# A 1-D convolution by Winograd points on one core: inputs laid out by channel blocks, output kept transposed, another order at the start

## The chip, the cores and the metric

The kernel runs on one core of a Trainium2 chip. TensorE (PE) multiplies matrices into PSUM, which has 8 banks of 512 fp32 values for each of 128 partitions. VectorE (DVE) and ScalarE (ACT) read PSUM; GpSimd (POOL) works on SBUF alone. SyncE (SP), ScalarE and GpSimd can issue DMAs. The metric is the device time of one execution in microseconds (us), the median of several runs.

## The reference

```python
B, S, C = 2, 2048, 1024          # x: (B, S, C), w: (3, C, C), all bf16
xp = jnp.pad(x, ((0, 0), (1, 1), (0, 0)))
y = sum(jnp.einsum('bsc,cd->bsd', xp[:, k:k + S, :], w[k]) for k in range(3))
y = (y - mean) * (g * (1.0 / jnp.sqrt(var + 1e-5))) + b
return jax.nn.silu(y)
```

It is a convolution of width 3 along the sequence with full channel mixing, then a normalization with given statistics and a SiLU.

## The kernel before

The convolution is computed in blocks of R = 6 output rows from NJ = 8 input rows by a Winograd scheme with eight points. For each batch, the sequence gives NB = 342 blocks. Three things are needed.

*Inputs.* A window of 128 rows of x, all 1024 channels, is loaded by `load_x` (L119, 2 KB for each row) and multiplied on TensorE by a small matrix `rm`. One matmul takes one window and one block of 128 channels and gives 8 points x 21 blocks = 168 columns, with the channels on the partitions. `t_job` (L314) does six or four such matmuls into two banks and has them evicted to `T_sb` by ScalarE (L333) or VectorE (L335), whichever its running estimates in `clock` say is done first. There are 17 windows for each batch and 8 channel blocks (`CT`). The matrix `rm` itself is built by some 20 small VectorE instructions (`transform_matrix`), the scale and bias of each channel come through four DMAs of GpSimd and a transpose.

*Weights.* For each block of 128 output channels (`dc`, 8 of them) the three taps w0, w1, w2 are combined to six tensors `u`: points 1 and 2 are (w0 + w2) plus and minus w1, points 3 and 4 (w0 + 4 w2) plus and minus 2 w1, points 5 and 6 (4 w0 + w2) plus and minus 2 w1. GpSimd does the last additions (L188, two for each pair), the sums come from VectorE (L169) or GpSimd (L167, L216, L225, L243), the doubled or quadrupled taps from ScalarE (L155, L237) or GpSimd. Points 0 and 7 (called 0 and inf) use w0 and w2 as they are ("raw", `wch` in the profile's names).

*Products.* A `Unit` (L344) is one output-channel block of one batch; there are 16, in the order (dc 0, batch 0), (dc 0, batch 1), (dc 1, batch 0) and so on. `product` (L361) is one point: 8 matmuls of 342 columns, one for each input-channel block, accumulated in one bank. A unit uses four banks, 0 to 3 or 4 to 7 in turn. `run` (L473) multiplies points 1, 3, 2, 4, 5, 6. Behind point 1, 3 and 5 ScalarE copies the bank to SBUF (`copy`, L380 and L382), since the next point that belongs to the pair is accumulated onto the same bank: point 2 onto point 1, 4 onto 3, 6 onto 5. VectorE then forms the sums and differences (`combine`, L387) into a few SBUF tiles and into the banks. At last points 0 and inf, the raw ones, are accumulated onto banks 0 and 3, and ScalarE applies scale, bias and SiLU (L394) into `yT`, which has the channels on the partitions.

The order of each engine's instructions is the order in which the program issues them (`manual_schedule` on all five engines). `run` has seams, `behind(1)` to `behind(6)`, at which work of other units is placed: the list `also` gives pairs of a seam and a function. `rest` (L465) puts the end of the unit before there: in the steady state the inner SiLUs and the product inf behind point 5, so between the matmuls of point 5 and point 6, and the product 0 behind point 6. The third unit (i = 2) has product 0 behind point 4 and inf behind point 5.

The first unit is special (`run_first`, L420): it multiplies points 0, 1, 3, 2, 4, 5, 6, and between its matmuls, at places given by the list `at` of `Between`, the transforms of batch 1 are issued into banks 4, 6 and 1. Its point inf and its SiLUs follow in the second unit (`rest_first`).

*Output.* A finished `yT` is turned by a DMA transpose (`turn`) and stored by seven DMAs on SP's queue. At the end the last unit is split into two halves of 214 and 128 blocks; there the transposes are done on TensorE (`put`, L530) and evicted (L531), and the products 0 and inf of the first half lie between points 5 and 6 of the second half and behind them.

Of the kernel before, what the change touches and what calls it, by code (L numbers as in the profile page):

```python
# [12 lines left out]
I32 = mybir.dt.int32  # L13
# [5 lines left out]
W0_AT = (5, 8, 16)  # L19
EARLY = 23  # L20
XBUFS = 12
T_FIRST = 21500.0
WARM = 2
WT = 21

@with_exitstack
def kernel(
    ctx: ExitStack,
    tc: tile.TileContext,
    x: bass.AP,  # L30
    w: bass.AP,
    mean: bass.AP,
    var: bass.AP,
    g: bass.AP,
    b: bass.AP,
# [3 lines left out]
    B, S, C = x.shape  # L39
    D = w.shape[2]  # L40
    CT, DC = C // P, D // P
    NB = -(-S // R)
    NW = -(-NB // WT)
    LAST = NB - WT * (NW - 1)
    assert S % P == 0 and NB <= 512
# [3 lines left out]
    wpool = ctx.enter_context(tc.tile_pool(name="wpool", bufs=1))  # L49
# [7 lines left out]
    opool = ctx.enter_context(tc.tile_pool(name="opool", bufs=2))  # L57
    xwin_scope = ExitStack()
    xpool = xwin_scope.enter_context(tc.tile_pool(name="xpool", bufs=XBUFS))
# [8 lines left out]
    rows = consts.tile([4 * DC, P], BF16, name="rows")  # L68
    zeros = consts.tile([P, 512], FP32, name="zeros")
    nc.vector.memset(zeros, 0.0)  # L70
    for _ in range(WARM):
        nc.tensor.matmul(ps[:, 7], lhsT=zeros[:, 0:P], rhs=zeros, start=True, stop=True)
# [4 lines left out]
    def transform_matrix():  # L77
        v = nc.vector
        val = consts.tile([P, 3, WT], I32, name="val")
        nc.gpsimd.iota(val, pattern=[[1, 3], [-R, WT]], base=-1, channel_multiplier=1)  # L80
        m = consts.tile([P, 4, 3, WT], FP32, name="m")
        f = consts.tile([P, 3, 2, WT], FP32, name="f")
        c = consts.tile([P, 2, WT], FP32, name="c")
        rm = consts.tile([P, NJ, WT], BF16, name="rm")
        m0, m2, m4, m6 = (m[:, q] for q in range(4))
        for q, coef in ((1, -8.0), (2, 1.0), (3, 1.0), (0, 36.0)):
            v.tensor_scalar(m[:, q], val, float(2 * q), coef, op0=ALU.is_equal, op1=ALU.mult)
        for k, (c4, c6) in enumerate(((34.0, -8.0), (40.0, -32.0), (10.0, -2.0))):
            v.scalar_tensor_tensor(out=f[:, k], in0=m4[:, 1:3], scalar=c4, in1=m2[:, 1:3], op0=ALU.mult, op1=ALU.add)
        v.scalar_tensor_tensor(out=c, in0=m6[:, 0:2], scalar=-36.0, in1=m0[:, 0:2], op0=ALU.mult, op1=ALU.add)  # L90
        for k, (c4, c6) in enumerate(((34.0, -8.0), (40.0, -32.0), (10.0, -2.0))):
            v.scalar_tensor_tensor(out=f[:, k], in0=m6[:, 1:3], scalar=c6, in1=f[:, k], op0=ALU.mult, op1=ALU.add)
        v.scalar_tensor_tensor(out=c, in0=m4[:, 0:2], scalar=189.0, in1=c, op0=ALU.mult, op1=ALU.add)
        f1, f2, f3 = (f[:, k] for k in range(3))
        for j, a0, s0, a1, op in (
            (1, f1[:, 0], 1.0, f1[:, 1], ALU.add), (2, f1[:, 0], 1.0, f1[:, 1], ALU.subtract),
            (3, f2[:, 1], 2.0, f2[:, 0], ALU.add), (4, f2[:, 1], -2.0, f2[:, 0], ALU.add),
            (5, f3[:, 0], 2.0, f3[:, 1], ALU.add), (6, f3[:, 0], 2.0, f3[:, 1], ALU.subtract),
            (0, m2[:, 1], 23.625, c[:, 1], ALU.add), (7, m2[:, 0], -23.625, c[:, 0], ALU.subtract),
        ):  # L100
            v.scalar_tensor_tensor(out=rm[:, j], in0=a0, scalar=s0, in1=a1, op0=ALU.mult, op1=op)
        return rm

    rm = transform_matrix()

    clock = {"pe": 3500.0, "act": 0.0, "dve": 0.0, "dma": 3600.0}
    cost = {"act": (0.833, 250.0), "dve": (1.042, 215.0)}
    bank_free = {}

    def ends(e, size):  # L110
        return max(clock[e], clock["pe"] + 100.0) + cost[e][0] * size + cost[e][1]

    def busy(e, size):
        clock[e] = ends(e, size)

    order = [NW - 1] + list(range(2, NW - 1)) + [0, 1]
    xwin = {}

    def load_x(bi, wi):  # L119
        xw = xpool.tile([P, C], BF16, name="xw")  # L120
        lo = max(R * WT * wi - 1, 0)
        hi = min(lo + P, S)
        nc.sync.dma_start(out=xw[0:hi - lo, :], in_=x[bi, lo:hi, :])  # L123
        clock["dma"] += 5.4 * (hi - lo)
        xwin[bi, wi] = xw, clock["dma"]

    w_all = w.rearrange("k (ct p) d -> p k ct d", p=P)
    raw, wts = {}, {}

    wpools = {0: wpool}  # L130

    def load_w(pair, k, half=None):

        if (pair, "tile") not in raw:
            raw[pair, "tile"] = wpools[pair % 2].tile([P, 3, CT, 2, P], BF16, name=f"wch{pair % 2}")
        wch = raw[pair, "tile"]
        h0, h1 = (0, 2) if half is None else (half, half + 1)
        cols = slice((2 * pair + h0) * P, (2 * pair + h1) * P)
        nc.sync.dma_start(
            out=wch[:, k, :, h0:h1].rearrange("p c h d -> p c (h d)"), in_=w_all[:, k, :, cols]  # L140
        )
        clock["dma"] += 1400.0 * (h1 - h0)
        for h in range(2):
            raw[2 * pair + h] = wch[:, :, :, h]

    double, sums, act_work, dve_work = {}, {}, [], []
# [5 lines left out]
    def double_w(dc, eng):  # L152
        t = spool.tile([P, CT, P], BF16, name="w1x2")
        if eng is nc.scalar:
            nc.scalar.mul(t, raw[dc][:, 1], 2.0)  # L155
            busy("act", CT * P)
        else:
            eng.tensor_scalar(t, raw[dc][:, 1], 2.0, 0.0, op0=ALU.mult, op1=ALU.add)
        double[dc] = t

    def even_part(dc, q, eng, by=None):

        w0, w2 = raw[dc][:, 0], raw[dc][:, 2]
        e = epool.tile([P, CT, P], FP32, name=f"e{q}")
        f, h = (w2, w0) if q == 1 else (w0, w2)
        if q == 0:
            eng.tensor_tensor(e, w0, w2, op=ALU.add)  # L167
        elif eng is nc.vector:
            eng.scalar_tensor_tensor(out=e, in0=f, scalar=4.0, in1=h, op0=ALU.mult, op1=ALU.add)  # L169
        else:  # L170
            t = spool.tile([P, CT, P], BF16, name="w1x2")
            if by is nc.scalar:
                by.mul(t, f, 4.0)
                busy("act", CT * P)
            else:
                by.tensor_scalar(t, f, 4.0, 0.0, op0=ALU.mult, op1=ALU.add)
            eng.tensor_tensor(e, t, h, op=ALU.add)
        if eng is nc.vector:
            busy("dve", CT * P)
        sums[dc, q] = e  # L180

    def transform_w(dc, q, signs=(0, 1)):

        o = double[dc] if q else raw[dc][:, 1]
        if (dc, q) not in wts:
            wts[dc, q] = upool.tile([P, 2, CT, P], BF16, name=f"u{q}")
        for i in signs:
            nc.gpsimd.tensor_tensor(wts[dc, q][:, i], sums[dc, q], o, op=(ALU.add, ALU.subtract)[i])  # L188

    def prepare_w(dc):  # L190

        even_part(dc, 0, nc.gpsimd)
        transform_w(dc, 0)

        def second():
            even_part(dc, 1, nc.vector)
            transform_w(dc, 1)

        def third():
            even_part(dc, 2, nc.vector)  # L200
            transform_w(dc, 2)

        act_work.append(lambda: double_w(dc, nc.scalar))
        dve_work.extend((second, third))

    def prepare_first(dc):


        w0, w2 = raw[dc][:, 0], raw[dc][:, 2]
        g, f = (spool.tile([P, CT, P], BF16, name="w1x2") for _ in range(2))  # L210
        nc.gpsimd.tensor_scalar(f, w0, 4.0, 0.0, op0=ALU.mult, op1=ALU.add)
        for q, t, h in ((0, w0, w2), (1, g, w0)):
            if q:
                nc.gpsimd.tensor_scalar(g, w2, 4.0, 0.0, op0=ALU.mult, op1=ALU.add)
            sums[dc, q] = epool.tile([P, CT, P], FP32, name=f"e{q}")
            nc.gpsimd.tensor_tensor(sums[dc, q], t, h, op=ALU.add)  # L216

        def left():
            transform_w(dc, 0, (0,))
            double_w(dc, nc.scalar)  # L220
            transform_w(dc, 1, (0,))
            transform_w(dc, 0, (1,))
            transform_w(dc, 1, (1,))
            sums[dc, 2] = epool.tile([P, CT, P], FP32, name="e2")
            nc.gpsimd.tensor_tensor(sums[dc, 2], f, w2, op=ALU.add)  # L225
            transform_w(dc, 2)

        return left

    def prepare_second(dc):  # L230

# [3 lines left out]
        def times4(tap):  # L235
            t = spool.tile([P, CT, P], BF16, name="w1x2")
            nc.scalar.mul(t, tap, 4.0)  # L237
            busy("act", CT * P)
            return t

        def even(q, t, h):
# [102 lines left out]
    class Unit:  # L344

# [383 lines left out]
```

## Time and profile before

| What | us |
|---|---|
| median of 3 runs (lowest, highest) | 187.62 (187.03, 187.85) |
| span of the profiled execution | 185.5 |
| PE busy | 178.0 |
| DVE busy | 153.0 |
| ACT busy | 112.9 |
| POOL busy | 146.8 |

The span goes from the first to the last instruction or landing that the profiler recorded. An engine's busy time is the union of its instructions; matmuls overlap each other, so the distance between their starts tells more than their own duration (299 ns for a spacing of about 145 ns). "Idle before, releaser" is the idle time ahead of an instruction and what ended it. Tile names such as `T_sb`, `u`, `wch`, `pc`, `ps` are those of the code. A line of a listing in order of time has the start, the length from the first to the last of the merged instructions, engine, line, operation, output and input, and a count. A line of windows has the stretch, its length, and for PE, weight loads, DVE, ACT and POOL the busy time and the number of instructions, then the granted clock, the DMA engines' busy share and GB/s.

### The profile page before, as it was taken

What the parts mean: (1) busy time and instruction counts of PE and PEld (TensorE: products, weight loads), DVE (VectorE), ACT (ScalarE), POOL (GpSimd) and SP (SyncE); (2) the same over time, 40 slices, a digit from 0 to 9 for tenths busy, and PEclk for the clock granted to TensorE, in tenths of its full rate; (3) what the DMA queues carried; (4) which work ended last, traced back from release to release, by engine and by line L of the source; (5) the groups of instructions that cost most, each with busy time, mean ns of one, the idle gap of its engine ahead of it and who ended that gap; (6) DMA issues with size and microseconds to landing.
All of it is one profiled execution on the core that took longest, in us unless ns stands there. A gap on an engine that the chain in (4) does not pass through costs nothing.

```text
span 185.5 us, 3732 instructions
## 1 busy us (share of the span) xinstructions
PE 178.0 (96%) x1403; PEld 125.9 (68%) x1403; DVE 153.0 (82%) x214; ACT 112.9 (61%) x183; POOL 146.8 (79%) x89
## 2 busy tenths in 40 slices
PE   6889999999999999999999999999999999999991
PEld 2678688866666666666666666666666666669890
DVE  5278777997668999999988998879988997678792
ACT  3589888896638565456545654565456546363791
POOL 7099899999998879999999999999999973020120
PEclk9999999999999999999999999999999999999998
DMA  5999999065426855698859557995583968766845
GB/s 166 326 344 328 377 386 252 7 203 143 79 48 62 183 106 134 198 200 187 161 114 206 109 135 156 217 211 108 136 178 80 209 57 203 151 139 134 196 96 113
DMA packets 88046, 31.72 MB, mean 171 GB/s; under 512 B 75659, under 2 KB 83866, under 8 KB 88028
## 3 DMA queue, kind: packets, MB, share of 16 engines
q1 hardware_dynamic: 86860, 31.24, 72.3%
q10 hardware_dynamic: 848, 0.20, 0.5%
q8 instruction: 11, 0.18, 0.4%
q0 software_dynamic: 320, 0.03, 0.2%
q14 instruction: 7, 0.06, 0.1%
HBM read 14.82 MB, written 8.39 MB: 125 GB/s over the span
## 4 chain that ended last, share of the span: by engine, by line
PE 85%; DMA 5%; DVE 4%; ACT 2%; SPq 1%; issue 0%; DVEq 0%; ACTq 0%
PE ps L369 79%; DMA xw<-in_x_dram 5%; PE ps L322 5%; DVE T_sb L335 3%; SPq L123 1%; ACT T_sb L333 1%; PE ps L530 1%; DVE sd L387 0%; DVE o L531 0%; ACT outer L394 0%; DVEq L335 0%; ACTq L333 0%
## 5 line engine op out<-in xcount | busy, mean ns | idle before, releaser
L369 PE MATMUL ps<-T_sb,u 128*128 128x342 bf16 (+2 forms) x816 | 120.1, 299 | 0.1
L369 PEld LDWEIGHTS <-u 128*128 128x128 bf16 x816 | 76.8, 97 | 33.4 <-issue 0.2
L188 POOL TENSOR_TENSOR u<-e,w1x 128x1024 bf16<-128x1024 f32 x32 | 69.4, 2191 | 3.9 <-DVE e L169 2.5
L369 PE MATMUL ps<-T_sb,wch 128*128 128x342 bf16 (+2 forms) x272 | 42.6, 299 | 0.4 <-ACT T_sb L333 0.4
L394 ACT ACTIVATE yT<-ps,beta,scale 128x342 bf16<-128x342 f32 (+4 forms) x49 | 33.5, 713 | 13.3 <-PE ps L369 13.3
L387 DVE SCALAR_TENSOR_TENSOR t<-ps,sd 128x684 f32<-128x684 f32 (+2 forms) x51 | 39.1, 822 | 0.6
L188 POOL TENSOR_TENSOR u<-e,wch 128x1024 bf16<-128x1024 f32 x16 | 38.5, 2424 | 1.2 <-DMA wch<-in_w_dram 0.7
L369 PEld LDWEIGHTS <-wch 128*128 128x128 bf16 x272 | 25.7, 97 | 11.9 <-issue 0.6
L380 ACT COPY pc<-ps 128x342 f32<-128x342 f32 (+2 forms) x35 | 14.9, 426 | 28.7 <-PE ps L369 28.4
L333 ACT CAST T_sb<-ps 128x1008 bf16<-128x1008 f32 (+2 forms) x31 | 25.6, 874 | 7.4 <-PE ps L322 7.1
L335 DVE CAST T_sb<-ps 128x1008 bf16<-128x1008 f32 (+2 forms) x19 | 20.7, 1116 | 10.4 <-PE ps L322 10.3
L387 DVE SCALAR_TENSOR_TENSOR ps<-ps,t 128x684 f32<-128x684 f32 (+2 forms) x34 | 28.3, 832 | 0.6
L169 DVE SCALAR_TENSOR_TENSOR e<-wch 128x1024 f32<-128x1024 bf16 x12 | 26.2, 2182 | 0.0
L322 PE MATMUL ps<-rm,xw 128*128 128x168 bf16 (+2 forms) x272 | 25.0, 237 | 1.0 <-ACT T_sb L333 0.3
L322 PEld LDWEIGHTS <-xw 128*128 128x128 bf16 (+2 forms) x272 | 20.9, 100 | 6.4 <-issue 3.7
L387 DVE SCALAR_TENSOR_TENSOR ps<-ps,pc 128x342 f32<-128x342 f32 (+2 forms) x34 | 16.9, 497 | 9.2 <-PE ps L369 7.8
L167 POOL TENSOR_TENSOR e<-wch 128x1024 f32<-128x1024 bf16 x7 | 16.9, 2409 | 0.4 <-DMA wch<-in_w_dram 0.4
L394 ACT ACTIVATE yT<-t,beta,scale 128x684 bf16<-128x684 f32 (+2 forms) x17 | 15.7, 924 | 0.0
L387 DVE SCALAR_TENSOR_TENSOR t<-ps,t 128x684 f32<-128x684 f32 (+2 forms) x17 | 13.9, 818 | 0.0
L589 POOL DMA_DIRECT2D out_dram<-o x2 | 1.3, 659 | 15.6 <-DMA o<-yT 15.6
L387 DVE SCALAR_TENSOR_TENSOR sd<-pc,ps 128x342 f32<-128x342 f32 (+2 forms) x17 | 8.2, 485 | 6.2 <-ACT sd L380 6.1
L380 ACT COPY sd<-ps 128x342 f32<-128x342 f32 (+2 forms) x17 | 7.3, 428 | 9.7 <-PE ps L369 9.1
(62 smaller groups left out, 61.8 us busy)
## 6 DMA issues: line engine op xcount, KB each, us to landing
xw<-in_x_dram SPq DMA_DIRECT2D x32, 256.0 KB
out_dram<-o SPq DMA_DIRECT2D x28, 192.0 KB
wch<-in_w_dram SPq DMA_DIRECT2D x8, 512.0 KB
wch<-in_w_dram SPq DMA_DIRECT2D x8, 256.0 KB
out_dram<-o SPq DMA_DIRECT2D x14, 120.0 KB
out_dram<-o SPq DMA_DIRECT2D x3, 128.0 KB
o<-yT SPq DMA_TRANSPOSE x15
out_dram<-o SPq DMA_DIRECT2D x12, 7.5 KB
```

The costliest lines, as they stand in the source:

```text
L123: nc.sync.dma_start(out=xw[0:hi - lo, :], in_=x[bi, lo:hi, :])
L167: eng.tensor_tensor(e, w0, w2, op=ALU.add)
L169: eng.scalar_tensor_tensor(out=e, in0=f, scalar=4.0, in1=h, op0=ALU.mult, op1=ALU.add)
L188: nc.gpsimd.tensor_tensor(wts[dc, q][:, i], sums[dc, q], o, op=(ALU.add, ALU.subtract)[i])
L322: nc.tensor.matmul(v[:, q, c], lhsT=xw[0:rows, (c0 + c) * P:(c0 + c + 1) * P], rhs=mat[0:rows, :, 0:n], start=True, stop=True,)
L333: nc.scalar.copy(dst, src)
L335: nc.vector.tensor_copy(dst, src)
L369: nc.tensor.matmul(self.bank[q], lhsT=lhsT, rhs=T_sb[self.bi][:, ct, j, nsl], start=not add and ct == 0, stop=ct == CT - 1, skip_group_che ...
L380: nc.scalar.copy(dst, self.bank[q])
L387: nc.vector.scalar_tensor_tensor(out=out, in0=in0, scalar=scalar, in1=in1, op0=ALU.mult, op1=op1)
L394: nc.scalar.activation(dst, src, ACT.Silu, bias=beta[:, dc:dc + 1], scale=scale[:, dc:dc + 1])
L530: nc.tensor.transpose(v[:, a, q], src, ident)
```

## The change

The arrays are laid out on the host before the launch, with no arithmetic beyond padding and the constant matrix: x as windows by batch and channel block, so that one channel block of 16 windows (512 KB) is one DMA with 4 KB for each partition; the last 48 rows of each batch apart (`xl`); w by output-channel block with 6 KB for each partition (2 KB for one tap); the four parameter vectors as one array; and the transform matrix as an input. The output stays as the device writes it, (batch, dc, channel, row in block, block), and is put in order on the host.

On the device, a transform job (`Jobs.do`) is now one channel block and six or four windows, so batch 0 is transformed channel block by channel block, through all eight banks in four pairs; batch 1 uses three pairs. While batch 0 is awaited, short matmuls of zeros (`keep_busy`) may be issued. The first unit (`First`) uses banks 0 and 1 for points 0, inf, 1, 3, 2, 4 (0 and inf are copied to `kept` and added later), then bank 2 for points 5 and 6; its matmuls and the transforms of batch 1 are issued in the order in which the running estimates say that they can start. Its point 6, its last combinations and its three SiLUs, from SBUF tiles, are placed in the second unit, at seams 1 to 4, together with ScalarE's scalings of the taps of dc 1 (`prepare_second`) at seams 1, 2 and 4. The third unit has both raw products at seam 4. Each unit's `yT` is stored by one DMA. The end has no transposes, and the inner SiLUs of the first half stand at seam 3 of the second half. In unchanged functions (`product`, `copy`, `combine`, `run`) the instructions are the same.

```diff
+    def keep_busy(until, bank):
...
+        z = zeros.bitcast(BF16)
+        n = 384 if clock["pe"] > WARM_AT else 192
+        while clock["pe"] + 200.0 < until:
+            nc.tensor.matmul(ps[:, bank, 0:n], lhsT=z[:, 0:P], rhs=z[:, 0:n], start=True, stop=True)
+            matmuls(n)
...
+        def evens():
+            even(dc, 0, w0, w2)
+            g = scaled(w2, 4.0, nc.gpsimd)
+            even(dc, 1, g, w0)
...
         def left():
+            double_w(dc, nc.vector)
...
+            for q, i in ((0, 0), (1, 0), (0, 1), (1, 1)):
+                transform_w(dc, q, (i,))
...
+            f = scaled(w0, 4.0, nc.gpsimd)
+            even(dc, 2, f, w2)
...
+            for i in range(2):
+                transform_w(dc, 2, (i,))
...
     def prepare_second(dc):
...
         def second():
+            even(dc, 1, scaled(w2, 4.0, nc.scalar), w0)
         def third():
             double_w(dc, nc.scalar)
             transform_w(dc, 1)
         def fourth():
+            even(dc, 2, scaled(w0, 4.0, nc.scalar), w2)
             transform_w(dc, 2)
...
+    class Jobs:
+        def __init__(self, bi):
...
+            self.todo = [(None, 0, 0)] + [
+                (ct, f, min(6, NF - f)) for ct in range(CT) for f in range(0, NF, 6)
+            ]
...
+        def place(self):
...
+            slots = [(4, 5), (6, 7), (2, 3)]
+            if not self.bi:
+                slots += [(0, 1)]
...
+    class First(Unit):
...
+            self.todo = [
+                (j, q, add, ct) for j, q, add in (
+                    (0, 0, False), (NJ - 1, 1, False), (1, 1, False), (3, 0, False), (2, 1, True), (4, 0, True),
+                    (5, 2, False), (6, 2, True),
+                ) for ct in range(CT)
+            ]
...
+        def at(self):
...
+            if q == 2 and jobs[1]:
+                return float("inf")
+            return max(u, t_at[self.bi, ct], bank_free.get(q, 0.0))
...
+        def finish(self):
+            while self.todo:
                 self.do()
+            b2, b3 = self.bank[2:]
+            self.combine(b3, b2, -0.5, self.p[5])
+            for t, a in zip(self.t, (-1.6, -0.4, -0.1)):
+                self.combine(t, self.high, a, t)
...
+        def rest(self, between):
+            return [(1, self.finish)] + [(q + 2, lambda q=q: self.silu(slice(2 * q, 2 * q + 2), self.t[q])) for q in range(3)]
...
+    load_small(0)
+    load_x(0, 0, 2)
+    for ct in range(1, CT):
+        load_x(0, ct)
+        if ct in W0_AT:
+            load_w(0, ((0, 2, 1)[W0_AT.index(ct)],))
...
+    while jobs[0]:
+        slot, ready = jobs[0].place()
+        keep_busy(ready, slot[0])
+        jobs[0].do()
...
+    unit = First(0, 0)
+    while jobs[1] or unit.todo[0][0] != 6:
+        if left and clock["dve"] > raw_at[0, 1] - 500.0:
+            left.pop()()
+        at = jobs[1].place()[1] if jobs[1] else None
+        if at is not None and (not unit.todo or at <= max(clock["pe"], unit.at())):
+            jobs[1].do()
+        else:
+            unit.do()
...
+        also = prev.rest(quiet)
+        if i == 1:
+            also = [(1, second[1]), (2, second[2]), (4, second[3])] + also
+        if i == 2:
+            also = prev.rest(quiet, 4, 4)
...
+        if bi == 0 and dc + 3 < DC:
+            load_w(dc + 3, (0, 1, 2))
+        prev.store(nc.sync)
...
+    h0.run(quiet, prev.rest(quiet, 5, 5))
+    prev.store(sp)
+    h1 = Unit(dc, bi, 0, 0, H)
+    h1.run(quiet, [(3, h0.silu_inner)])
+    h0.store(sp, inner)
+    h0.product(3, NJ - 1, True, quiet)
+    h0.product(0, 0, True, quiet)
+    h1.product(0, 0, True, quiet)
+    h1.product(3, NJ - 1, True, quiet)
+    h0.silu(outer, ps[:, h0.b0:h0.b0 + 4:3, H:NB])
     h1.silu_inner()
+    h1.silu(0, h1.bank[0])
+    h1.silu(R - 1, h1.bank[3])
+    h0.store(sp, outer)
+    h1.store(sp, slice(0, R - 1))
+    h1.store(ac, slice(R - 1, R))
```

More of the change, by code (lines that the diff above doesn't have):

```diff
@@ L104 @@
[L104 to L144, printed above, removed]
@@ L146, with ends, busy, landed @@
-    double, sums, act_work, dve_work = {}, {}, [], []
+    clock = {"pe": 3400.0, "act": 3200.0, "dve": 1500.0, "pool": 2500.0, "dma": 2300.0}
+    cost = {"act": (0.833, 170.0), "dve": (1.042, 155.0), "pool": (2.0, 80.0)}
+    def ends(e, size, ready):
+        return max(clock[e], ready) + cost[e][0] * size + cost[e][1]
+    def busy(e, size, ready=None):
+        clock[e] = ends(e, size, clock["pe"] + 250.0 if ready is None else ready)
+        return clock[e] + 100.0
+    def landed(nbytes):
+        left = nbytes
+        slow = max(0.0, 8200.0 - clock["dma"]) * 255.0
+        at = min(left, slow)
+        clock["dma"] += at / 255.0 + (left - at) / 410.0
+        return clock["dma"] + 100.0
@@ new lines, in matmuls, with load_small @@
+    def matmuls(cols):
+        clock["pe"] += cols / (2.34 if clock["pe"] > WARM_AT else 1.18)
+    def keep_busy(until, bank):
[4 more added lines that the diff above has]
+            matmuls(n)
+    xt, xt_at, raw, raw_at = {}, {}, {}, {}
+    small, small_at = {}, {}
+    def load_small(bi):
+        t = xpool.tile([P, NF, P], BF16, name="xw").rearrange("p f c -> p (f c)")
+        nc.sync.dma_start(out=t[0:LROWS, 0:CT * P], in_=xl[bi])
+        small[bi], small_at[bi] = t, landed(LROWS * CT * P * 2)
@@ new lines, in load_x, with load_w @@
+    def load_x(bi, ct, parts=1):
+        t = xpool.tile([P, NF, P], BF16, name="xw")
+        xt[bi, ct], xt_at[bi, ct] = t, []
+        step = NF // parts
+        for q in range(parts):
+            s = slice(q * step, (q + 1) * step)
+            nc.sync.dma_start(out=t[:, s], in_=x[bi, ct, :, s])
+            at = landed(P * step * P * 2)
+            xt_at[bi, ct] += [at] * step
+    def load_w(dc, taps):
+        if dc not in raw:
+            raw[dc] = wpools[dc // 2 % 2].tile([P, 3, CT, P], BF16, name=f"wch{dc // 2 % 2}")
+        if len(taps) == 3:
+            nc.sync.dma_start(out=raw[dc], in_=w[dc])
+        else:
+            for k in taps:
+                nc.sync.dma_start(out=raw[dc][:, k], in_=w[dc, :, k])
+        for k in taps:
+            raw_at[dc, k] = landed(P * CT * P * 2)
@@ L204, in prepare_w, with pool @@
         dve_work.extend((second, third))
+    def pool(n=1):
+        clock["pool"] += n * 2130.0
+        return clock["pool"]
+    u_at = {}
     def prepare_first(dc):
         w0, w2 = raw[dc][:, 0], raw[dc][:, 2]
[L210 to L216, printed above, removed]
@@ L344, with quiet @@
+    def quiet():
+        pass
+    yts = [ypool.tile([P, R, NB], BF16, name=f"yT{q}") for q in range(B)]
     class Unit:
@@ L705 @@
[L705 to L709 removed]
+    inner, outer = slice(1, R - 1), slice(0, R, R - 1)
+    h0 = Unit(dc, bi, 4, H, NB)
+    h0.run(quiet, prev.rest(quiet, 5, 5))
[6 more added lines that the diff above has]
+    h1.product(0, 0, True, quiet)
```

577 lines of the change are left out of this document (209 added, 368 removed), and 8 rows, old and new, of the table _POINTS.

## The prediction

> **What bounds the kernel now.** I read the page first, then the chain that ended last, then windows, and then the order of time around the seams. The page says that TensorE is busy nearly always, at the full granted clock:
>
> ```profile
> PE 178.0 (96%) x1403; PEld 125.9 (68%) x1403; DVE 153.0 (82%) x214; ACT 112.9 (61%) x183; POOL 146.8 (79%) x89
> PEclk9999999999999999999999999999999999999998
> ```
>
> The chain shows from where on it is the bound alone: 952 matmuls in one piece from 37.44 us. What can be won or lost lies before that piece and behind it. A load takes 5.54 us from issue to landing while the queues are full, and eight 128-wide matmuls at the end take 0.45.
>
> ```profile
> 8.13 5.54 DMA xw<-in_x_dram
> ...
> 37.44 136.02 PE ps L369 x952
> ...
> 179.80 0.45 PE ps L369 x8
> ...
> 180.95 0.57 ACT outer L394
> ```
>
> The window over the middle gives the pace (691 records touch it, some 689 start in it: 100/689 = 0.1451 us for a 342-wide matmul); two single microseconds give the loading rate with x alone in 2 KB rows (387 GB/s) and with weights in 512 B rows (274).
>
> ```profile
> 60.00:160.00 100.00, 100.00 (x691) 66.85 (x690) 91.85 (x110) 54.21 (x92) 90.50 (x39) 1.00 0.75 155
> 24.00:25.00 1.00, 1.00 (x13) 0.81 (x12) 0.54 (x1) 0.99 (x2) 1.00 (x1) 1.00 1.05 387
> 29.00:30.00 1.00, 1.00 (x14) 0.90 (x13) 0.61 (x1) 1.00 (x3) 0.92 (x2) 1.00 1.22 274
> ```
>
> Last, ScalarE and GpSimd in the second unit. See the spacing of ScalarE's instructions (a copy 0.35, a doubling 0.96, a SiLU of 684 elements 0.85) and that its copy of point 5 has only 0.35 us of slack; GpSimd's last line ends the second channel block's weights, at 53.16.
>
> ```profile
> 36.79 0.45 ACT L380 COPY pc<-ps 128x342 f32<-128x342 f32 x1 [0.42 <-PE ps L369]
> 36.55 0.89 PE L322 MATMUL ps<-rm,xw 127*128 127x168 bf16 x10
> 37.29 7.13 PE L369 MATMUL ps<-T_sb,u 128*128 128x342 bf16 x48
> 42.52 1.06 ACT L237 ACTIVATE w1x<-wch 128x1024 bf16<-128x1024 bf16 x1
> 43.48 0.62 ACT L394 ACTIVATE yT<-ps,beta,scale 128x342 bf16<-128x342 f32 x1
> 44.45 0.44 ACT L380 COPY pc<-ps 128x342 f32<-128x342 f32 x1 [0.35 <-PE ps L369]
> 46.15 0.95 ACT L394 ACTIVATE yT<-t,beta,scale 128x684 bf16<-128x684 f32 x1
> 48.94 4.22 POOL L188 TENSOR_TENSOR u<-e,w1x 128x1024 bf16<-128x1024 f32 x2
> 54.70 7.13 PE L369 MATMUL ps<-T_sb,u 128*128 128x342 bf16 x48
> ```
>
> **The mark.** Both kernels issue the same 1088 product matmuls and 272 transform matmuls. I count to one mark M, the first matmul of point 6 in the third unit: in both orders 168 products and all transforms lie before it. Before, M is 54.70. Behind it lie 792 wide matmuls (792 x 0.1451 = 114.9) and 48 narrow ones of the first half unit (0.09 each, 4.3): 119.2. Then 0.45 for eight transposes, and 11.04 from there (174.46) to the end: 185.4, against the profiled span of 185.5. The median of the runs is 187.62, so 2.1 us lie around the span; I keep them.
>
> **Start: loading.** Removed are the matrix built on VectorE, two identity matmuls, the parameter transposes and one fp32 warm-up: all end before 9 us, beside the first loads, and cost nothing now. The two new small DMAs on ScalarE's queue must land before the first transform; the nearest rows, GpSimd's small loads, land 3.3 to 5.1 us after issue. Late by 1 us, the transforms still catch up, as tiles 6 and 7 arrive last: 0. The eleven filler matmuls that the planner's list gives fit gaps; the last costs 0 to 0.2.
>
> The last tile of batch 0 has 4.87 MB through its end (4.29 of x, two weight taps, small ones). The first 4 us move 0.58 MB (53, 182 and 344 GB/s). Rows of 2 KB at 387 and 512 B at 274 mean 0.085 and 0.030 us on one of 16 engines; in a straight line 4 KB takes 0.157, an estimate of 416 GB/s. So 4 + 0.52/0.387 + 3.77/0.416 = 14.4 for the bytes. The load in the chain above landed 1.5 to 2.2 us after the bytes ahead of it had passed: 16.3 (15.9 to 16.6; at the mean rate of before up to 18).
>
> [...]
>
> First product: six matmuls 0.44, latency 0.25, ScalarE's eviction 1.01 (its row), 0.1: 18.1. From there to the end of point 5: 56 products, 8.1, and 128 transforms of 0.0725, 9.3 (batch 1). The corresponding stretch of before (19.61 to 37.44) took 1.4 more than its work; I keep 1.4 (0.5 to 2.5: evictions, two new copies, one more combination and the doubling on VectorE, which no row shows: between the 0.69 of a 1024-element copy and the 2.18 of the fp32 sum; I take 0.7, the nearest in kind). End of point 5: T = 36.9. The same 56 products end at 38.45 in before, 112 matmuls ahead of M. **Won: 1.5.**
>
> **Second and third unit: ScalarE.** Times now from T. The second unit puts on ScalarE, between its first copy and the copy of point 5: scaling of a tap, copy, doubling, SiLU, copy, SiLU, another scaling, SiLU. Before had neither the first scaling (done earlier) nor the three wide SiLUs there. The first copy starts at 1.41 (point 1, 8 x 0.1451 + 0.25), the scaling at 1.76; the next copy waits for point 3 until 3.73 (point 6 of the first unit now lies between). Then with the spacings shown: doubling 4.10, SiLU 5.07, copy 5.93, SiLU 6.28, scaling 7.14, SiLU 8.11, copy of point 5 8.97 to 9.41. Point 6 adds into the bank that this copy reads, so TensorE waits until 9.47; its own work brings it there at 6.97. **Lost: 2.5**, if the SiLUs' inputs are there: VectorE ends them at 3.9, 4.7 and 5.5. Queued behind the SiLUs are those very copies; nothing else of ScalarE waits.
>
> The third unit now runs both raw-weight products ahead of point 5, none between 5 and 6. The cover of its copy is gone: 0.25 + 0.44 + 0.06 = **0.75 lost**. The 36.55 to 37.29 rows show this wait: point 5 ends at 36.55, the copy runs 36.79 to 37.24, point 6 starts at 37.29, and ten transforms filled it. So M = 36.9 + 112 x 0.1451 (16.25) + 3.25 = 56.4.
>
> GpSimd gives a floor for M. Its chain from the first u to the last of the second channel block ran 19.24 to 53.16, plus a scaling of 1.1 now inside: 35.0. It starts when tap 2 (3.82 MB, 11.9 + 1.8) plus 5.5 of sums is done: 19.2. M is not before 54.2, so GpSimd isn't reached.
>
> **Middle.** The same instructions. Fifteen DMA transposes and the block stores go from SP's queue, one 525 KB store per unit comes; it queues behind a weight load that waits for the unit's raw products, but its tile is next written some 15 us later. Cost 0. The 15.6 us that GpSimd waited for transposes held nobody.
>
> **End.** From the end of the first half's point 6 (0): eight transposes less before it (0.45 won). Points 1, 3, 2, 4, 5 of the last half take 0.45 each, 0.13 wait for a copy: 2.4. The first half's inner SiLUs now stand ahead of the copy of point 5, and need VectorE until 2.27: the copy ends at 3.5, point 6 at 4.0 (1.2 wait, where before other products and transposes lay). Two products of 0.72, two of 0.45: TensorE ends at 6.3. ScalarE from 5.68: 0.61, 0.51, 0.46, 0.37, 0.46: 8.1. The last store: before took 3.0 from its issue (182.48, second of two) for 64 KB; 32 KB alone, between that and the 2.1 of the smallest: 2.75. 10.85 in place of 11.04. **Won: 0.65.**
>
> Sum: 56.4 + 119.2 + 10.85 = 186.45, against 185.4 by the same count: +1.05, and 188.7 for the median.
>
> **Rivals.** (1) Faster: loading ends so early that GpSimd's floor takes the place of ScalarE's wait. For it speaks that no row shows 4 KB rows; against it, that evictions then limit. With the tile at 15.0 and 0.5 of waits T is 34.7 and M 54.2: 184.3, so 186.5. It decides by itself from T below 34.9. Chance 0.17. (2) No change: the tile at 16.0, waits of 0.8 and a store of 2.4 give T 36.0, M 55.5, the end at 185.2: 187.4. 0.28. (3) The start gains nothing: the tile at 17.5 and waits of 2 give T 38.7, M 58.2: 188.3, so 190.5. 0.15. (4) The forecast, with waits of 1.3 to 2.3: 188.6 to 189.6. 0.40. [...]
>
> 0.5% (0.94 us) is about what these runs can tell from no change. Slower 0.40 + 0.15, same 0.28, faster 0.17. The range 185.9 to 190.5 reaches from most of (1) to (3); the forecast's own stands with it.
>
> **What would show it.** The first wide product near 18 and T near 37; TensorE idle for 2.5 us in the second unit with ScalarE's copy ending it, 0.75 in the third; M near 56.4; TensorE ending some 1.8 us ahead of ScalarE at the end. The prediction falls if the second unit shows no such wait, if T lies below 35, or if GpSimd's weights end the wait in the third unit.

## The result and the profile after

The changed kernel takes 193.93 us, the median of 4 runs (192.45 to 194.83), against 187.43 for the kernel before, run beside it. The ratio is 1.034, with a 95% interval of 1.029 to 1.039. Slower was forecast, but by 0.6%; 188.7 us and the range up to 190.5 were both too low. The profiled execution took 194.4 us with a span of 192.6; it was forecast by the same count at 186.45. So 6.15 us of that execution have to be explained, and they fall in three places. (Two of the kernels below have one run over 1.5% above their fastest, 195.25 and 188.58; it is left out of their medians and ratios.)

Two lines of the page of the changed kernel: PE's busy time is no longer than before (176.9 against 178.0), though the span is 7.1 us longer, and one digit in the row of the granted clock, the eleventh of 40, just behind a quarter of the span, is a 6.

```profile
PE 176.9 (92%) x1373; PEld 125.1 (65%) x1373; DVE 150.9 (78%) x192; ACT 109.0 (57%) x175; POOL 139.4 (72%) x73
PEclk9999999999699999999999999999999999999995
```

The chain that ended last in the changed kernel (start, length, what). TensorE's one piece of before, 136 us from 37.44, has become two: 64 matmuls from 47.75 and 840 from 59.40. The 840 are the middle and the first half unit, as long as predicted. The 64 should take 64 x 0.1451 = 9.3 us and took 11.08. The last SiLU ends at 184.24 + 2.35 = 186.59; the span ends 6.0 us later.

```profile
47.75 11.08 PE ps L340 x64
...
58.90 0.46 ACT pc L349
59.36 0.04 issue
59.40 119.51 PE ps L340 x840
...
182.12 2.09 PE ps L340 x24
184.21 0.02 issue
184.24 2.35 ACT yT L361 x5
```

Windows of the changed kernel; the last three columns are granted clock, DMA share and GB/s. Four things are to be seen. Loads of x in 4 KB rows moved 413 GB/s. From 48 to 51 us TensorE ran at a clock of 0.50: five or six matmuls touch each microsecond in place of nine in the window behind. The middle has the 691 records of before. At the end the bytes of the last stores are through soon after 188, and then nothing moves for 4 us, although the span isn't over.

```profile
10.00:14.00 4.00, 3.95 (x49) 3.44 (x47) 3.84 (x4) 3.62 (x6) 0.00 (x0) 1.00 1.03 413
48.00:49.00 1.00, 1.00 (x5) 0.59 (x4) 0.27 (x1) 0.00 (x0) 1.00 (x1) 0.50 0.79 320
49.00:50.00 1.00, 1.00 (x6) 0.47 (x4) 0.00 (x0) 0.00 (x0) 1.00 (x2) 0.50 0.51 205
50.00:51.00 1.00, 1.00 (x5) 0.58 (x4) 0.67 (x2) 0.00 (x0) 1.00 (x1) 0.50 0.00 0
51.00:52.00 1.00, 1.00 (x9) 0.60 (x7) 1.00 (x2) 0.12 (x1) 0.92 (x2) 0.96 0.04 8
60.00:160.00 100.00, 100.00 (x691) 66.84 (x690) 92.39 (x110) 53.18 (x91) 92.11 (x41) 1.00 0.27 88
...
187.00:188.00 1.00, 0.00 (x0) 0.00 (x0) 0.00 (x0) 0.00 (x0) 0.00 (x0) 0.81 0.70 173
188.00:189.00 1.00, 0.00 (x0) 0.00 (x0) 0.00 (x0) 0.00 (x0) 0.00 (x0) 0.50 0.11 24
189.00:190.00 1.00, 0.00 (x0) 0.00 (x0) 0.00 (x0) 0.00 (x0) 0.00 (x0) 0.50 0.00 0
```

The second unit in order of time, first ScalarE of the changed kernel. It is the queue that the prediction wrote down: copy, scaling, copy, doubling, SiLU, copy, SiLU, scaling, SiLU, copy. Only the second scaling did not start right behind the SiLU, but waited 0.48 until GpSimd had ended a sum at 45.43.

```profile
39.27 0.45 ACT L349 COPY pc<-ps 128x342 f32<-128x342 f32 x1 [1.01 <-PE ps L340]
39.61 1.06 ACT L145 ACTIVATE w1x<-wch 128x1024 bf16<-128x1024 bf16 x1
41.55 0.46 ACT L351 ACTIVATE pc<-ps 128x342 f32<-128x342 f32 x1 [0.87 <-PE ps L340]
41.90 1.05 ACT L145 ACTIVATE w1x<-wch 128x1024 bf16<-128x1024 bf16 x1
42.85 0.95 ACT L361 ACTIVATE yT<-t,beta,scale 128x684 bf16<-128x684 f32 x1
43.70 0.43 ACT L349 COPY sd<-ps 128x342 f32<-128x342 f32 x1
44.02 0.96 ACT L361 ACTIVATE yT<-t,beta,scale 128x684 bf16<-128x684 f32 x1
45.46 1.06 ACT L145 ACTIVATE w1x<-wch 128x1024 bf16<-128x1024 bf16 x1 [0.48 <-POOL e L155]
46.42 0.94 ACT L361 ACTIVATE yT<-t,beta,scale 128x684 bf16<-128x684 f32 x1
47.27 0.43 ACT L349 COPY pc<-ps 128x342 f32<-128x342 f32 x1
```

And TensorE in the same stretch. Point 5 of the first unit starts at 36.44 and ends 8 x 0.1451 later: T = 37.6. Point 6 of the second unit starts at 47.75, released by ScalarE's copy, where TensorE's own work would have brought it at 37.6 + 6.97 = 44.57. The last line is the mark M, 59.40.

```profile
36.44 1.33 PE L467 MATMUL ps<-T_sb,u 128*128 128x342 bf16 x8 [0.25 <-ACT T_sb L313]
...
40.19 4.80 PE L340 MATMUL ps<-T_sb,u 128*128 128x342 bf16 x32
47.75 7.58 PE L340 MATMUL ps<-T_sb,u 128*128 128x342 bf16 x40 [2.75 <-ACT pc L349]
...
59.40 2.77 PE L340 MATMUL ps<-T_sb,u 128*128 128x342 bf16 x18 [0.59 <-ACT pc L349]
```

The stores of the changed kernel (queue, count, size, median us from issue to landing). The last 32 KB, on a queue of its own, landed 5.0 us after issue; the prediction had 2.75.

```profile
out_dram<-yT SPq DMA_DIRECT2D x15, 513.0 KB, 6.7
...
out_dram<-yT SPq DMA_DIRECT2D x1, 160.0 KB, 5.2
...
out_dram<-yT ACTq DMA_DIRECT2D x1, 32.0 KB, 5.0
```

The terms against the prediction, all of the profiled execution:

| Term | predicted | measured | difference |
|---|---|---|---|
| T, end of point 5 of the first unit | 36.9 | 37.6 | +0.7 |
| wait in the second unit | 2.5 | 47.75 - 44.57 = 3.2 | +0.7 |
| lower clock behind it | none | 11.08 - 9.46 = 1.6 | +1.6 |
| wait in the third unit | 0.75 | 0.75 | 0 |
| M | 56.4 | 59.40 | +3.0 |
| M to the end of the first half's point 6 | 119.2 | 119.2 | 0 |
| from there to the end of ScalarE's work | 8.1 | 186.59 - 178.6 = 8.0 | -0.1 |
| from there to the end of the span | 2.75 | 192.6 - 186.59 = 6.0 | +3.2 |

(9.46 is the length of the same 64 matmuls at the full clock, from an experiment below. The prediction's tail is 8.1 + 2.75 = 10.85.)

### The profile page after: what moved, and what is told of

Read it like the earlier page. It is cut to its first block, busy times and chain, and to the rows that moved or that the text cites. A ratio compares the mean times of both kernels' runs of the same rounds, so it can differ in the third digit from the quotient of the medians.

```text
span 192.6 us, 3476 instructions
## 1 busy us (share of the span) xinstructions
PE 176.9 (92%) x1373; PEld 125.1 (65%) x1373; DVE 150.9 (78%) x192; ACT 109.0 (57%) x175; POOL 139.4 (72%) x73
## 2 busy tenths in 40 slices
DMA packets 8080, 23.55 MB, mean 122 GB/s; under 512 B 2592, under 2 KB 2592, under 8 KB 8064
## 4 chain that ended last, share of the span: by engine, by line
PE 69%; POOL 14%; DMA 5%; ACT 3%; issue 3%; SPq 2%; DVE 1%; DVEq 0%; ACTq 0%; POOLq 0%
PE ps L340 69%; POOL u L168 8%; POOL e L155 6%; DMA wch<-in_w_dram 5%; ACT yT L361 2%; SPq L119 2%; POOL w1x L147 1%; ACT pc L349 1%; DVE ps L356 1%; SPq L130 0%; DVE t L356 0%; SPq L110 0%; ACT w1x L145 0%; DVEq L356 0%; ACTq L349 0%
## 5 line engine op out<-in xcount | busy, mean ns | idle before, releaser
L340 PE MATMUL ps<-T_sb,u 128*128 128x342 bf16 (+2 forms) x768 | 111.4, 301 | 4.3 <-ACT pc L349 4.2
L340 PEld LDWEIGHTS <-u 128*128 128x128 bf16 x768 | 73.0, 98 | 38.6 <-issue 5.1
L340 PE MATMUL ps<-T_sb,wch 128*128 128x342 bf16 (+2 forms) x256 | 39.2, 299 | 0.0
L315 DVE CAST T_sb<-ps 128x1008 bf16<-128x1008 f32 (+1 forms) x19 | 20.8, 1113 | 11.2 <-PE ps L299 10.8
L356 DVE SCALAR_TENSOR_TENSOR ps<-ps,t 128x684 f32<-128x684 f32 (+2 forms) x32 | 26.5, 829 | 0.6
L299 PE MATMUL ps<-rm,xw 128*128 128x168 bf16 x256 | 23.6, 243 | 2.2 <-DMA xw<-in_x_dram 2.1
L155 POOL TENSOR_TENSOR e<-wch 128x1024 f32<-128x1024 bf16 x8 | 19.3, 2408 | 7.5 <-DMA wch<-in_w_dram 7.5
L299 PEld LDWEIGHTS <-xw 128*128 128x128 bf16 x256 | 20.3, 101 | 5.3 <-DMA xw<-in_x_dram 3.1
L361 ACT ACTIVATE yT<-t,beta,scale 128x684 bf16<-128x684 f32 (+2 forms) x19 | 17.6, 926 | 0.0
L351 ACT ACTIVATE pc<-ps 128x342 f32<-128x342 f32 (+2 forms) x16 | 7.0, 439 | 9.2 <-PE ps L340 6.9
```

The costliest lines, as they stand in the source:

```text
L155: nc.gpsimd.tensor_tensor(sums[dc, q], a, b, op=ALU.add)
L299: nc.tensor.matmul(src[:, q // per, q % per], lhsT=xt[self.bi, ct][:, f + q], rhs=rm, start=True, stop=True)
L315: nc.vector.tensor_copy(dst, src)
L340: nc.tensor.matmul(self.bank[q], lhsT=lhsT, rhs=T_sb[self.bi][:, ct, j, nsl], start=not add and ct == 0, stop=ct == CT - 1, skip_group_che ...
L351: nc.scalar.mul(dst, self.bank[q], by)
L356: nc.vector.scalar_tensor_tensor(out=out, in0=in0, scalar=scalar, in1=in1, op0=ALU.mult, op1=op1)
```

## The experiments

Three causes were put to the test: the order of ScalarE's queue (theory of the prediction), the fall of the clock behind the wait, and the landing of the last stores. The rivals were that GpSimd ends the wait anyway, that the lower clock belongs to the place and not to the idle time, and, for the stores, that the split over two queues makes them late.

### ScalarE's order in the second unit

```diff
-            return [(1, self.finish)] + [(q + 2, lambda q=q: self.silu(slice(2 * q, 2 * q + 2), self.t[q])) for q in range(3)]
+            return [(1, self.finish)] + [(n, lambda q=q: self.silu(slice(2 * q, 2 * q + 2), self.t[q])) for q, n in ((0, 2), (2, 3), (1, 5))]
...
-            also = [(1, second[1]), (2, second[2]), (4, second[3])] + also
+            also = [(1, second[1]), (2, second[2]), (6, second[3])] + also
```

> In the second unit ScalarE's scaling of tap 0 moves from seam 4 to seam 6 and the second of the first unit's SiLUs (tile t1) from seam 3 to seam 5, both behind the copy of point 5; nothing else changes. Theory: that queue on ScalarE made TensorE wait 3.1 us, and the granted clock fell to 0.5 because of this idle time (3.3 us at half pace, 1.8 us lost). Then the wait falls to about 0.75, the clock stays at 1.0, and the mark M (first matmul of point 6 in the third unit, 59.40 in the changed kernel) comes to 55.4 by TensorE's own work, or to 56.1 if GpSimd's last weights (ready at 56.1) take over the wait. Span 189.3, time some 3.2 us below the changed kernel's. Rival: the clock falls for another reason (time since the start, load); then only 2.4 us of the wait go, the rows after 48 us still show 0.5, and M is 57 or later.

TensorE's order in this kernel: point 6 of the second unit started at 44.41 with the 0.59 of an uncovered copy, the clock stayed full, and M came at 54.64, as early as in the kernel before (54.70). What ended the wait at M is now GpSimd, as the prediction's floor for M (54.2) has it.

```profile
44.41 5.97 PE L340 MATMUL ps<-T_sb,u 128*128 128x342 bf16 x40 [0.59 <-ACT pc L349]
...
54.64 7.14 PE L340 MATMUL ps<-T_sb,u 128*128 128x342 bf16 x48 [0.75 <-POOL u L168]
...
81.20 1.32 PE L340 MATMUL ps<-T_sb,wch 128*128 128x342 bf16 x8 [0.73 <-DVE ps L356]
```

M is 4.8 us earlier than in the changed kernel. Of this, 2.4 is the shorter wait (0.75 in place of 3.2) and 1.4 the stretch from point 6 to M (10.23 in place of 11.65). The other 0.9 is an earlier start, which the edit doesn't touch: point 5 of the first unit ends at 36.7 in place of 37.6. GpSimd's last sum was early as well, at 54.6 in place of 56.1. Yet the span is only 2.5 us shorter (190.1), and the median 1.5 (192.41; ratio to before 1.027, 1.021 to 1.033). The last line above is a new wait: VectorE, which forms the later blocks' weight sums between its combinations, is the chain from 57 to 81 us and holds TensorE for 0.73; from M to ScalarE's end it is 128.2 in place of 127.2. And ScalarE ended at 182.84, 7.25 us ahead of the end: in this execution the last store was later still.

```profile
out_dram<-yT SPq DMA_DIRECT2D x15, 513.0 KB, 7.5
...
out_dram<-yT ACTq DMA_DIRECT2D x1, 32.0 KB, 6.2
```

So the order of ScalarE's queue makes the wait, as predicted; of the 4.8 us at M, 1.0 goes to VectorE and 1.25 to the last store.

### The idle time filled

Sixteen matmuls of zeros, into a bank that is free there, between points 5 and 6 of the second unit. They are work added; nothing else is changed.

```diff
+            for _ in range(self.fill):
+                nc.tensor.matmul(ps[:, 0, 0:NB], lhsT=zb[:, 0:P], rhs=zb[:, 0:NB], start=True, stop=True)
...
+        unit.fill = 16 if i == 1 else 0
```

> 16 matmuls of zeros (2.3 us) are put on TensorE between points 5 and 6 of the second unit, into a bank that nobody uses then; the wait for ScalarE's copy stays as it is. Theory: the idle time lowers the granted clock; with it filled the clock stays at 1.0, point 6 still starts near 47.7, M comes 1.8 us earlier (57.6), span 190.8. Rival: the clock falls for another reason, or zeros do not count as activity: M stays at 59.4 and the time is that of the changed kernel, 193.9.

TensorE's order in this kernel: point 6 starts at 47.64, as late as in the changed kernel, but its 40 matmuls take 5.96 in place of 7.58, and M is 57.68 in place of 59.40.

```profile
44.75 2.48 PE L421 MATMUL ps<-zeros 128*128 128x342 bf16 x16
47.64 5.96 PE L344 MATMUL ps<-T_sb,u 128*128 128x342 bf16 x40 [0.41 <-ACT pc L353]
...
57.68 6.55 PE L344 MATMUL ps<-T_sb,u 128*128 128x342 bf16 x44 [0.59 <-ACT pc L353]
```

So the lower clock belongs to the idle time, and costs 1.6 us. One execution alone would not show it, since the clock doesn't fall behind every such gap (see below); but in all four kernels whose gap here is filled or 0.6 us short it stayed full. The median hardly shows the gain (193.38; ratio 1.032, 1.027 to 1.036), since here too the end gave the gain back: 7.55 us from ScalarE's end to the end of the span.

The length of the idle time alone does not decide it. Behind TensorE's idle 2.2 to 2.8 us in this place the clock fell to 0.50 in 5 of 7 profiled executions (the changed kernel and six kernels below that differ from it in the output alone) and not in two: it fell behind 2.16 us (one store) and stayed full behind 2.56 (768 bytes). It fell between 0.1 us ahead of the first matmul of point 6 and 0.9 us behind it, and stayed at 0.50 for 3.4 us in the four executions whose windows reach to its end; the 40 matmuls of point 6 took 7.58 to 7.64 us in all five, in place of 5.97. It stayed full where the idle time was 0.6 or filled, and behind 1.43 us in the loading of the changed kernel (1.00 from 8 to 9 us; the sixteen matmuls from 8.38 took 1.33).

### The end: how the output's rows lie in memory

One store for all rows of the last half, on SP's queue, in place of two on two queues:

```diff
-    h1.store(sp, slice(0, R - 1))
-    h1.store(ac, slice(R - 1, R))
+    h1.store(sp)
```

> The last half's six rows are stored by one DMA on SyncE's queue in place of five rows there and the last on ScalarE's queue. If the late landing came from two queues at once, the last landing comes 2 to 3 us earlier and the time is about 191.5. If it is the pieces themselves, the end moves by less than 1 us (later rather than earlier, since all six rows wait for the last SiLU): 193.5 to 194.9.

194.86 us, ratio 1.037 (1.030 to 1.044). ScalarE ended at 187.24 and the span at 193.2: 6.0 us, as with two stores. The two queues aren't the cause.

Rows of the output 768 bytes apart in place of 684; the 342 blocks written are the same, and so is the work on the engines:

```diff
-    NB = out.shape[4]
+    NB = 342
...
-_OUTS = [((2, 8, 128, 6, 342), "bfloat16")]
+_OUTS = [((2, 8, 128, 6, 384), "bfloat16")]
...
-    got = _np.asarray(r.results[0]["out_0_dram"])
+    got = _np.asarray(r.results[0]["out_0_dram"])[..., 0:342]
```

> The output array in HBM has rows of 384 blocks (768 B) in place of 342 (684 B), so that every row starts at a multiple of 256 B; the same blocks are stored, and the padding is cut on the host. Theory: the last stores' bytes are out by 188.1 and 4.5 us more pass until the end because pieces of 256 B at odd addresses are slow to complete; with starts at multiples of 256 B that falls to some 1.5 us, as before, and the span is about 189.7, the time 3 us below the changed kernel's. Rival: the late landing comes from the number of pieces or from the two queues; then the end stays 6 us behind the last issue and the time stays within 0.5 us of 193.9.

190.09 us, ratio 1.015 (1.010 to 1.019): 3.8 us less than the changed kernel. The stores of this kernel:

```profile
out_dram<-yT SPq DMA_DIRECT2D x15, 513.0 KB, 3.8
...
out_dram<-yT SPq DMA_DIRECT2D x1, 160.0 KB, 2.2
...
out_dram<-yT ACTq DMA_DIRECT2D x1, 32.0 KB, 2.0
```

Every store lands earlier, and the span ends 3.0 us behind ScalarE's work, near the 2.75 of the prediction. In the profiled execution the clock happened to stay full behind the wait as well, so neither of the two terms that the prediction lacked is in it. The chain of this kernel:

```profile
46.28 9.46 PE ps L340 x64
...
56.32 119.51 PE ps L340 x840
```

M is 56.32 (predicted 56.4), the span 186.5 (predicted 186.45) and the time of this execution 188.28 (predicted 188.7). That it is so close is in part luck: T is 0.3 earlier than predicted (36.6), the wait in the second unit 0.2 longer (2.7) and the last store 0.25 later. The other three runs of this kernel took 189.75 to 190.72; the clock can't be read from them by place, only as a mean (0.985, 0.986 and 0.995 of full, 0.995 in the profiled one).

What of the 84 bytes matters? Four more distances, with the same edit and another number for 384, told the start address from the gap between rows.

> Rows of 385 blocks (770 B): as much padding as with 768 B, but the starts fall on odd multiples of 2 B again. If the start address of a piece is what makes its landing late, the landings go back to 6 to 7 us for a whole unit (3.8 with 768 B) and the last one to 5 us or more, and the time goes back to 193 to 195. If it was the pitch, or that rows no longer touch each other, the time stays near 190.1.

> Rows of 352 blocks (704 B = 11 x 64 B). If multiples of 64 B are enough, the landings and the time are those of 768 B rows (a unit 3.8 us, the last piece 2.0, 190.1). If only multiples of 256 B help, most rows are late and the time is 192 to 194.

> The output's rows lie 748 bytes apart (374 blocks, 342 of them written), so that starts are multiples of 4 bytes as in the changed kernel (684), but 64 bytes lie between one row's end and the next row's start. Theory 'touching': what makes the landings late is that neighbouring rows share a piece of memory of some tens of bytes; then the landings are those of the runs with 704 and 770 bytes: a unit's store 4.8 to 4.9 us, the last 32 KB 2.0 to 2.8, from the last SiLU's end to the end of the span 3.0 to 3.9, time 190.5 to 192.5. Rival 'start address': the odd starts do it; then the landings are those of the changed kernel: a unit's store 6 to 7 us, the last 32 KB 5, the span 6 us behind the last SiLU, time 193 to 194.5.

> The output's rows lie 1024 bytes apart (512 blocks, 342 of them written), so that every row starts at a multiple of 512 bytes, against 256 in the run with 768 bytes. If alignment beyond 256 bytes adds nothing, the landings are those of 768 bytes: a unit's store 3.8 us, the last 32 KB 2.0, 3.0 us behind the last SiLU, time 189.5 to 190.7. If the longer pitch costs (the same bytes over a third more memory), a unit's store takes 4.5 us or more and the time is above 191; if 512 bytes help further, a unit's store takes under 3.3 and the last 32 KB under 1.7.

| Rows apart, bytes | gap between rows | unit's store, us | 160 KB | last 32 KB | ScalarE's end to span's end | median | ratio to before (95%) |
|---|---|---|---|---|---|---|---|
| 684 (changed kernel) | 0 | 6.7 | 5.2 | 5.0 | 6.0 | 193.93 | 1.034 (1.029, 1.039) |
| 704 = 11 x 64 | 20 | 4.8 | 2.2 | 2.0 | 3.0 | 190.76 | 1.016 (1.011, 1.020) |
| 748 | 64 | 5.4 | 3.2 | 3.2 | 4.3 | 191.94 | 1.022 (1.016, 1.027) |
| 768 = 12 x 64 | 84 | 3.8 | 2.2 | 2.0 | 3.0 | 190.09 | 1.015 (1.010, 1.019) |
| 770 | 86 | 4.9 | 3.0 | 2.8 | 3.85 | 192.43 | 1.026 (1.023, 1.028) |
| 1024 = 16 x 64 | 340 | 4.1 | 2.2 | 2.0 | 3.0 | 192.09 | 1.024 (1.017, 1.032) |

The stores of the kernel with 748 bytes, whose rows have the same kind of start as in the changed kernel (a multiple of 4 bytes) and only the gap is new:

```profile
out_dram<-yT SPq DMA_DIRECT2D x15, 513.0 KB, 5.4
...
out_dram<-yT ACTq DMA_DIRECT2D x1, 32.0 KB, 3.2
```

As far as one profiled execution of each tells, the gap alone takes 1.7 of the 3.0 us off the end; a distance that is a multiple of 64 bytes takes the other 1.3, and with such a distance neither the size of the gap (20, 84 or 340 bytes) nor a higher power of two changes the last stores. Whether a multiple of 8, 16 or 32 bytes would do as well was not tried: 748 and 770 are multiples of none of them. The 770 bytes, whose starts are multiples of 2 alone, land no later than the 748. So neither theory holds alone: rows that touch are the larger part, the distance between the starts the smaller. For the unit's store there is a second difference: without a gap six rows of a channel go as one packet (8,080 packets in the execution, 17,680 with a gap: 9,600 more, which is 15 stores x 128 channels x 5). For the last stores the packets are the same with all six distances, so packet size isn't their cause. Why such stores land late was not tried further and stays open, the more so as the last half's pieces begin 428 bytes into their rows in every kernel.

With 1024 bytes the stores land as with 768, and yet the time is 2.0 us longer. In its profiled execution the whole of it lies ahead of M: M is 59.33 against 56.32 and the spans differ as much (189.5 and 186.5), with 9.46 us for the 64 matmuls in both. T is 38.9 against 36.6, and the other 0.7 passes in the second unit, where TensorE first idled 0.94 for an eviction by VectorE. Its first product came at 21.03 us, that of the 768 at 18.61. Whether its longer output has to do with that isn't shown: over all profiled executions with the changed kernel's loads the first product came between 17.94 and 21.03 us.

In the changed kernel the bytes of the last stores were through by 189, and the span ended at 192.6. With how the rows lie, the end of the span comes between 3.0 and 6.0 us behind ScalarE's end in the table.

### Both edits, and a kernel faster than both

ScalarE's order and 768 bytes together:

> ScalarE's order of the first experiment together with rows of 768 B. Theory: the two costs are separate, so M is 54.6 to 56.1 (GpSimd's weights) and the end 130.2 later, as with 768 B alone: span 184.8 to 186.3, time 186.6 to 188.2, the kernel before within 0.5%. If they share a cause, the sum of the two single gains is not reached and the time is above 189.

188.64 us (188.44 to 189.19), ratio 1.007 (1.005 to 1.009): 0.4 above the range expected. The gains add up: point 6 waits 0.59, the clock stays full, the span ends 3.0 us behind ScalarE. What was left is GpSimd's floor at M and the wait of 0.72 for VectorE, here at 81.82. M in TensorE's order of this kernel, and what it waited for in GpSimd's:

```profile
55.27 7.14 PE L340 MATMUL ps<-T_sb,u 128*128 128x342 bf16 x48 [0.69 <-POOL u L168]
```

```profile
51.00 4.22 POOL L168 TENSOR_TENSOR u<-e,w1x 128x1024 bf16<-128x1024 f32 x2
```

GpSimd's last addition ended at 55.22, and M came right behind. So four things were added. GpSimd quadruples tap 0 while it waits for tap 2; two taps are loaded one block earlier; the third unit has one raw product between points 5 and 6 again; and so has the last half, which covers the copy with the first half's products:

```diff
-W0_AT = (4, 5, 7)
+W0_AT = (3, 4, 7)
...
+            nc.gpsimd.tensor_scalar(self_f, w0, 4.0, 0.0, op0=ALU.mult, op1=ALU.add)
             even(dc, 0, w0, w2)
...
-            f = scaled(w0, 4.0, nc.gpsimd)
-            even(dc, 2, f, w2)
+            even(dc, 2, early[0], w2)
...
-            also = prev.rest(quiet, 4, 4)
+            also = prev.rest(quiet, 5, 4)
...
-    h1.run(quiet, [(3, h0.silu_inner)])
+    h1.run(quiet, h0.rest(quiet, 5, 6))
     h0.store(sp, inner)
-    h0.product(3, NJ - 1, True, quiet)
-    h0.product(0, 0, True, quiet)
...
-    h0.silu(outer, ps[:, h0.b0:h0.b0 + 4:3, H:NB])
```

> In addition: GpSimd quadruples tap 0 before tap 2 is there and both taps are loaded one tile earlier (its chain then ends 2.4 us earlier, below 54), the third unit has product inf between points 5 and 6 again (0.6 to 0.75 less), and in the last half the first half's inner SiLUs and product inf stand between points 5 and 6 and its product 0 behind 6, as in the kernel before (some 1.3 us less at the end). Theory: M = T + 16.25 + 0.75 = 54.0 with T 37.0, the end 129 later: span 183, time 185, faster than the kernel before by 1.3%. Rival: the start varies so much with the loads (T 36.7 to 39.1 so far) that it stays within 0.5%.

186.27 us, ratio 0.995 (0.993 to 0.997): faster than the kernel before by half a per cent, and than the changed one by 7.7 us. 185 was expected; T was 37.7, not 37.0, so the rival named there, a start that varies, took the rest. The chain of this kernel has TensorE in one piece from 45.38, as the kernel before had from 37.44; M is 54.66 (GpSimd had ended at 53.6), and ScalarE's SiLUs end at 180.74, 3.07 us before the end of the span at 183.8.

```profile
45.38 128.83 PE ps L344 x904
...
176.77 3.97 ACT yT L365 x8
```

M is where it was in the kernel before (54.70), so the whole gain is behind it: 183.8 - 54.66 = 129.1 us, 130.8 before. The wait for VectorE near 81 us is gone too; which of the four edits took it away was not separated.

## Why the prediction was wrong

*Start.* Right in its parts, short in its sum. The 416 GB/s estimated for 4 KB rows were reached from 10 to 15 us (413 on average, 399 to 428 in single microseconds, against the 387 of before), so the straight line through the two kinds of rows held there. The core moved 379 on average from 4 to 16 us, but from 4 to 10 us only 357. TensorE idled for x 1.43 us at 8.38 and 0.46 at 16.53, the last tile of batch 0 was there at 17.8 and not at 16.3, and the first product came at 19.74, not 18.1. T was 37.6 (36.9): of the 1.5 us won, 0.85 stayed. The stretch from the first product to T took 17.9 us and not 18.8, so its waits were overestimated by as much (0.5 in place of 1.4), and that hid over half of the miss.

*Second unit.* The mechanism, its place and its releaser were right, and the first experiment shows it. The size was 3.2 in place of 2.5: the later of the two scalings also waited 0.48 for GpSimd to end a sum, which the chain of spacings had left out by asking only whether the SiLUs' inputs were there.

*The missing term behind it.* The step "Lost: 2.5" took idle time at its length. Behind it TensorE ran at half clock until 51 us, 1.6 us more, which no row shown of before could tell, as its TensorE runs in one piece from 37.44 us on.

*Third unit.* 0.75 predicted, 0.75 measured (0.59 of idle time and the latency of the last matmul). GpSimd wasn't reached, as forecast, but its floor was set too early: its last sum ended at 56.1 here, and at 54.6 to 56.1 in the ten executions with the changed kernel's loads, not at 54.2. A floor of 56.1 leaves the predicted M of 56.4 a margin of 0.3 us and not of 2.2, so that this part came out right is in part luck.

*Middle.* Right: the same records in the same 100 us. The unit's stores took 6.7 us each, and nobody waited for them.

*End.* Up to the end of ScalarE's work right to 0.1 us: point 6 of the last half started at 182.12 and so ended 4.0 behind the end of the first half's, as predicted (the wait 1.1 against 1.2). **The step that failed is its last term, the last store at 2.75 us.** It measured 6.0. The two rows that it stood between were stores of the old layout: of before, the second of ScalarE's two last stores, issued some 0.5 us behind the first and landed at 185.5, and the smallest of GpSimd's.

```profile
181.97 1.02 ACTq L541 DMA_DIRECT2D out_dram<-o  x2
...
out_dram<-o POOLq DMA_DIRECT2D x3, 0.5 KB, 2.1
```

So the bounds allowed nothing above 3.0; a new layout of the output was no different to them than a new size. The prediction treated the output's new form as fifteen transposes saved, and never asked what its rows do at the receiving end.

Of the 6.15 us, 3.2 are this store, 1.6 the clock, 0.7 each the start and the longer wait. None of the rivals had the clock or the store. The range could not hold them, because it was made of the loading, the waits of the start and a last store of 2.75 us at most.

## What to carry to other kernels

A new layout in memory changes the stores' price as well as the loads': where the last store ends the span, its landing is bounded from both sides with the layout as an unknown, and rows that are padded to a multiple of 64 bytes are worth a try (3 us here at the end of the span). An idle gap of TensorE such as the 2.2 to 2.8 us here is priced with the time behind it, since the clock may fall (to 0.50 in 5 of 7 executions here, at 1.6 us in the changed kernel), and a few matmuls of zeros in the gap tell, over several executions, whether it does. And a gain ahead of a late landing shows in the chain before it shows in the time: compare marks such as M, not medians, to see what an edit did.

## What the runs showed that was not expected

The same store of 32 KB landed in 2.0 us or in 5.0 to 6.2, by the distance of the rows that it writes alone. In the four profiled executions with rows of 684 bytes the two in which ScalarE ended earlier landed later behind it: with ScalarE's end at 187.24, 186.59, 184.86 and 182.84 the span ended 6.0, 6.0, 7.55 and 7.25 us behind; whether this is a rule or chance wasn't tried. And matmuls of no use, put into an idle gap, made the useful ones behind them faster by 1.6 us.
